# Both heads' sums turned into one tile, two score columns made by ScalarE, and a new list of due times, in an attention and two-layer MLP kernel

## The chip, the cores and the metric

The kernel runs on one core of one Trainium2 chip. The metric is the device time of one execution in microseconds. Engines are named as in the profile: PE is TensorE (PEld its weight loads), DVE is VectorE, ACT is ScalarE, POOL is GpSimd, SP is SyncE, which issues nearly all DMAs here.

## The reference

Attention over 4 batches, 8 heads, 576 positions, head dimension 64, in which scores more than `tau` under the row's maximum are cut off; then two MLP blocks over 2304 tokens (512 wide, 2048 hidden), the first with a squared ReLU, the second with a sigmoid gate.

```python
scores = scale * np.matmul(q, k.transpose(0, 1, 3, 2))
thresh = np.max(scores, axis=-1, keepdims=True) - tau
scores = np.where(scores >= thresh, scores, -1e9)
scores = scores - np.max(scores, axis=-1, keepdims=True)
attn = np.exp(scores)
attn = attn / (np.sum(attn, axis=-1, keepdims=True) + 1e-09)
out = np.matmul(attn, v)
# x = the heads side by side, (2304, 512)
r = np.maximum(x @ w_in, 0.0);  x = (s * (r * r) + b) @ w_out
h = x @ w2_in;  y = (h * (1.0 / (1.0 + np.exp(-1.702 * h)))) @ w2_out
```

## The kernel before

The kernel writes out no order of its own. Its functions hand steps to a planner (`Plan.add`, L133): each step names the engines that may run it with a cost in ns, what it reads and writes, and a due time. `Plan.run` (L175) then lays the steps out one engine at a time by due time and dependence, and buffers of one tag are handed out strictly in the order in which the program asked for them. A step's due time is that of its group plus 100 ns times the group's entry in the list `MOVES` (L53, 663 entries, one a group). TensorE steps of the attention fall due 282.77 us earlier than that (`first`).

Attention runs in 32 head pairs: for each batch (4) and each half of its queries (a unit: 256 queries, in the second unit 64 more, the "last" part), four pairs of heads. The two units of batch 0 are in fp32 and the other six in float16 pieces (value and remainder). A pair has four or five score tiles of 128 queries by 576 keys. For a tile TensorE forms negated scores in two PSUM banks (L563); VectorE takes the minimum `nm` (L587); a step forms `tb`, in float16 tiles two columns, the bound and the bias of the exponential (L601, VectorE; in fp32 tiles L595, one column, GpSimd); ScalarE takes the exponential (L609); VectorE masks it and sums it (L613). Then the tile is turned: fp32 by TensorE (L624) and copies (L393), float16 by two ScalarE and GpSimd steps (L393, L637) and a transposing DMA.

At the end of a pair, `finish_sums` inverts the sums (L649) and spreads them along the queries so that a column of `rs` scales a column of the product with V. In the first 16 pairs this is done through the one PSUM bank of tag `T`: for each head two transpositions (L677) and one copy of 64 partitions (L393), and in units with a last part a third transposition (L683) and two small copies into `rm` (L688). In the other 16 pairs the sums go through DRAM. The product with V (L708) takes the same bank, and VectorE scales it out of PSUM (L723, L729). `finish_last` does the same for the last 64 queries (L749, L757).

The weights of both blocks are converted tile by tile (`convert`, L838): a load of 512 KB into one of three buffers `wst`, a cast (L393 on ScalarE or L387 on VectorE) and a VectorE step that joins two pieces (L851). The first block of 256 tokens goes through the first MLP in fp32 (`pair32`, L1117 to L1133; `rows32`, L1151), as soon as its attention is through; its affine step `s*r*r+b` is a ScalarE step (L1133). The other blocks use float16 pieces (`pair` L1090, `bank` L1183). When attention has ended its memory goes to the second MLP, which forms seven products in place of eight for each 2 by 2 of quarters (`hidden7` L1416, `rows7` L1483 and L1504) over four blocks of 512 tokens and a last one of 256, made of the 64 last queries of each batch. `out` in `rows7` (L1534, L1538) writes the result; for the last block that is two stores for each of two tiles, all issued by SyncE (L415).

Of the kernel before, what the change touches and what calls it, by code (L numbers as in the profile page):

```python
# [121 lines left out]
class Plan:  # L122
# [4 lines left out]
    HOP = {("PE", "PE"): 0.0, ("DVE", "DVE"): 125.0, ("DVE", "SP"): 125.0, ("POOL", "POOL"): 105.0, ("POOL", "SP"): 60.0}  # L127
# [197 lines left out]
def act(cols, psum=False):  # L325
    return cols * 0.834 + (53.0 if psum else 93.0)
# [12 lines left out]
class Kernel:  # L339
# [229 lines left out]
    def tile_step(self, p, i):  # L569
# [22 lines left out]
        if plain:  # L592
            add(
                {"POOL": 360.0},
                lambda _: nc.gpsimd.tensor_scalar(tb(), nm.ap, self.under, None, ALU.add), [nm], [both],  # L595
                prio=self.plan.prio - KN["tb"] * pace,
            )
        else:
            add(
                {"DVE": Shared(200.0)},  # L600
                lambda _: nc.vector.tensor_scalar(both.ap, self.offs, nm.ap, None, ALU.add), [nm], [both],  # L601
                prio=self.plan.prio - KN["tb"] * pace,
            )
# [38 lines left out]
    def finish_sums(self, p):  # L642
# [8 lines left out]
        p["rs"] = rs = self.at("rs", [P, n], F32)  # L651
        if p["last"]:
            p["rm"] = rm = self.at("rm", [P, H2], F32)
        if p["spread"]:
# [7 lines left out]
            for t, part in ((rs, main), (p.get("rm"), last))[: 1 + p["last"]]:  # L662
                cols = t.shape[1]
                for h in range(2):
                    self.load(
                        lambda t=t, h=h: t[h * H2 : (h + 1) * H2],
                        lambda part=part, h=h, cols=cols: rd[part][h * cols : (h + 1) * cols].partition_broadcast(H2),
                        [(t, h)], H2 * cols * 4, reads=[rd],
                    )
            return  # L670
        for h in range(2):
            rT = self.ps("T", [H2, n])

            def turn(_, h=h, rT=rT):
                for t in range(T):
                    i = T * h + t
                    nc.tensor.transpose(rT[:, t * P : (t + 1) * P], ri[:, i : i + 1].to_broadcast([P, H2]), self.ident)  # L677
            add({"PE": pe(2 * T, P)}, turn, [ri], [rT])
            self.copy(lambda h=h: rs[h * H2 : (h + 1) * H2], lambda rT=rT: rT.ap, [rT], [(rs, h)], n, psum=True, more=90.0)
        if not p["last"]:  # L680
            return
        mT = self.ps("T", [P, P])
        add({"PE": pe(2, P)}, lambda _: nc.tensor.transpose(mT.ap, ri[:, 2 * T : 2 * T + 1].to_broadcast([P, P]), self.ident), [ri], [mT])  # L683

        def pick(_):
            for h in range(2):
                rows = slice(h * H2, (h + 1) * H2)
                nc.scalar.activation(rm[rows], mT[rows, rows], AF.Copy)  # L688
        add({"ACT": 220.0}, pick, [mT], [rm])
# [9 lines left out]
    def finish_main(self, p):  # L699
# [18 lines left out]
        x, hp = p["rs"], p["hp"]  # L718
        xs = self.x_of(p["unit"])
        if p["unit"] < KN["fu"]:  # L720
            add(
                {"DVE": dve(n, psum=True) + 60},
                lambda _: nc.vector.tensor_tensor(xs[:, hp, :], Up.ap, x.ap, ALU.mult), [Up, x], [(xs, (0, hp))],  # L723
# [5 lines left out]
            lambda _: nc.vector.scalar_tensor_tensor(x.ap, Up.ap, vb[:, sc : sc + 1], x.ap, ALU.mult, ALU.mult),  # L729
            [Up, vb, x], [x],  # L730
        )
        self.split(
            lambda: xs[:, 0, hp, :], lambda: xs[:, 1, hp, :], lambda: x.ap, [x], [(xs, (0, hp)), (xs, (1, hp))], n, on=None,
        )

    def finish_last(self, p):
# [7 lines left out]
        mT, rm = self.ps("T", [P, H2]), p["rm"]  # L744

        def mix(_):
# [10 lines left out]
            lambda _: nc.vector.scalar_tensor_tensor(xm.ap, mT.ap, sc(), rm.ap, ALU.mult, ALU.mult),  # L757
            [mT, rm] + [vb] * (not p["f32"]), [xm],
# [346 lines left out]
    def pair32(self, u, jp):  # L1105
# [22 lines left out]
        if jp % 2 == 0:  # L1128
            u["g"].append(Buf(self.wp, "g", [P, CH, n], F32, KN["g"]))
        g, k = u["g"][-1], 2 * (jp % 2)  # L1130
        add(
            {"ACT": act(512) + 186},
            lambda _: nc.scalar.activation(  # L1133
                g[:, k : k + 2, :].rearrange("p a b -> p (a b)"), gt.ap, AF.Identity, bias=self.b_ap, scale=self.s_ap
            ),
            [gt, self.scal], [(g, k)],
        )
# [619 lines left out]
```

## Time and profile before

| | before |
|---|---|
| median of 3 runs | 1010.17 us (1006.05 to 1010.31) |
| the profiled execution | 1013.42 us, its span 1011.5 us |
| mean granted TensorE clock | 0.994 |
| busy: TensorE, its weight loads | 971.5 us (96%), 755.0 us (75%) |
| busy: VectorE, ScalarE, GpSimd | 763.6 us (75%), 659.1 us (65%), 251.9 us (25%) |
| chain that ended last | TensorE 74%, VectorE 12%, DMA 6%, ScalarE 5% |

A share of the whole span mixes stages: attention, first MLP and second MLP overlap and have different limits. So the rows further below take the span in stretches, and name what TensorE waited for in each.

### The profile page before, as it was taken

The numbers are of one execution on the slowest core, as the hardware profiler recorded it, in microseconds if no ns is written. First come the engines' busy times: TensorE is split into PE (matmuls) and PEld (weight loads), VectorE is DVE, ScalarE is ACT, GpSimd is POOL, SyncE is SP. The second block draws the span as 40 slices with busy tenths as digits, with TensorE's granted clock in tenths as the row PEclk, the third lists the DMA queues.
The fourth block names the chain that finished last, engine by engine and source line by source line (L and its number), as shares of the span: only waits on it lengthen the run. The fifth ranks groups of instructions, "written<-read, shape, count | busy, mean of one in ns | idle before, by whom it ended". The sixth has DMA issues, their size and how long they took to land.

```text
span 1011.5 us, 22501 instructions
## 1 busy us (share of the span) xinstructions
PE 971.5 (96%) x8649; PEld 755.0 (75%) x8649; DVE 763.6 (75%) x1752; ACT 659.1 (65%) x1349; POOL 251.9 (25%) x362
## 2 busy tenths in 40 slices
PE   6889997999999999999999999999999999999997
PEld 3455665777788777788778888887687687687695
DVE  6989788887687775686665698989859577859665
ACT  5778875597675665776556588787448266547464
POOL 2101134335344544334453101210302000201001
PEclk9999999999999999999999999999999999999999
DMA  7877276785678666667655346601011000010000
GB/s 262 290 267 234 83 150 150 150 194 122 121 147 197 157 136 130 139 143 150 119 128 101 93 137 206 222 12 42 2 42 43 12 32 19 25 43 21 22 23 22
DMA packets 173067, 115.93 MB, mean 115 GB/s; under 512 B 136536, under 2 KB 149920, under 8 KB 172960
## 3 DMA queue, kind: packets, MB, share of 16 engines
q1 hardware_dynamic: 172960, 114.50, 44.0%
q8 instruction: 68, 1.11, 0.5%
q14 instruction: 39, 0.32, 0.1%
HBM read 72.62 MB, written 10.00 MB: 82 GB/s over the span
## 4 chain that ended last, share of the span: by engine, by line
PE 74%; DVE 12%; DMA 6%; ACT 5%; issue 2%; SPq 1%; POOL 0%; DVEq 0%; ACTq 0%
PE a L1483 9%; PE a L1416 9%; PE yy L1183 9%; PE yy L1090 7%; PE S L563 7%; PE y L1090 5%; PE T L708 5%; PE a L1504 3%; PE d L1504 3%; PE y L1183 3%; PE yy L1416 3%; PE y L1151 2%; PE d L1416 2%; DMA wst<-in_moe_w_in 2%; DVE l L967 2%
## 5 line engine op out<-in xcount | busy, mean ns | idle before, releaser
L637 POOL TENSOR_TENSOR p<-e,p 128x512 f16<-128x512 f32 x108 | 129.1, 1195 | 203.9 <-ACT p L393 150.2
L1090 PEld LDWEIGHTS <-wb 128*128 128x128 f16 x1536 | 148.8, 98 | 27.8 <-issue 10.0
L1183 PEld LDWEIGHTS <-wb 128*128 128x128 f16 x1536 | 147.4, 98 | 25.9 <-issue 9.0
L1416 PEld LDWEIGHTS <-l 128*128 128x128 f16 x1680 | 150.7, 98 | 18.8 <-issue 1.5
L1183 PE MATMUL yy<-g,wb 128*128 128x256 f16 x1248 | 145.8, 273 | 0.7 <-ACT gt L1097 0.7
L587 DVE TENSOR_REDUCE nm<-S 128x1 f32<-128x576 f32 x144 | 104.5, 750 | 42.7 <-PE S L563 42.3
L613 DVE SCALAR_TENSOR_TENSOR e<-S,tb,e 128x576 f32<-128x576 f32 x144 | 114.6, 812 | 27.0 <-ACT e L609 25.7
L609 ACT ACTIVATE e<-S,tb 128x576 f32<-128x576 f32 x108 | 76.4, 735 | 59.5 <-DVE tb L601 56.3
L1416 PE MATMUL a<-xs,l 128*128 128x256 f16 (+1 forms) x960 | 109.5, 262 | 1.1 <-ACT wb L1428 1.1
L1090 PE MATMUL yy<-xs,wb 128*128 128x256 f16 x888 | 107.1, 275 | 1.0 <-ACT gt L1208 1.0
L393 ACT ACTIVATE p<-e 128x576 f16<-128x576 f32 x108 | 73.0, 679 | 38.4 <-DMA PT<-p 21.6
L411 POOL TENSOR_TENSOR gt<-gt 128x256 f32<-128x256 f32 (+1 forms) x23 | 18.8, 822 | 267.9 <-DVE gt L411 200.7
L1090 PE MATMUL y<-xs,wb 128*128 128x256 f16 x648 | 77.2, 273 | 2.4 <-ACT gt L1097 1.2
L1504 PEld LDWEIGHTS <-g 128*128 128x128 f16 x714 | 69.5, 98 | 10.1
L395 ACT ACTIVATE g<-gt 128x256 f16<-128x256 f32 (+2 forms) x137 | 49.4, 394 | 30.7 <-DVE gt L411 19.8
L563 PE MATMUL S<-kk,qa 64*128 64x288 f32 (+1 forms) x320 | 55.3, 449 | 8.4 <-ACT kk L448 5.7
L563 PE MATMUL S<-kk,qb 64*128 64x288 f32 (+1 forms) x320 | 58.6, 462 | 3.1 <-DVE e L613 3.0
L1428 ACT ACTIVATE wb<-a 128x256 f32<-128x256 f32 (+1 forms) x120 | 41.4, 357 | 30.2 <-PE a L1416 28.1
L967 DVE SCALAR_TENSOR_TENSOR g<-gt,g 128x256 f16<-128x256 f32 (+1 forms) x133 | 58.0, 466 | 2.7 <-ACT g L395 2.5
L1340 ACT ACTIVATE gt<-wb,x2h 128x256 f32<-128x256 f32 (+2 forms) x80 | 44.4, 577 | 10.4 <-DVE wb L1435 9.7
L851 DVE SCALAR_TENSOR_TENSOR wb<-wst,tw 128x512 int32<-128x512 int32 x64 | 45.3, 719 | 5.2 <-ACT tw L393 4.7
L1483 PE MATMUL a<-wb,wst 128*128 128x512 f16 x216 | 48.9, 380 | 0.0
(202 smaller groups left out, 1786.1 us busy)
## 6 DMA issues: line engine op xcount, KB each, us to landing
wst<-in_moe_w_in SPq DMA_DIRECT2D x32, 512.0 KB, 4.8
wst<-in_moe_w_out SPq DMA_DIRECT2D x32, 512.0 KB, 4.5
rv<-in_v SPq DMA_DIRECT2D x32, 320.0 KB, 3.4
kk<-in_k SPq DMA_DIRECT2D x32, 288.0 KB, 2.9
qb<-in_q SPq DMA_DIRECT2D x16, 288.0 KB, 3.3
yd<-gt SPq DMA_DIRECT2D x18, 256.0 KB, 2.6
wb<-yd SPq DMA_DIRECT2D x16, 256.0 KB
out<-gt SPq DMA_DIRECT2D x16, 256.0 KB, 2.0
```

Source lines behind the costliest of these rows:

```text
L393: nc.scalar.activation(dst(), src(), AF.Copy)
L563: nc.tensor.matmul(Sp[to, half, :HALF], q[h][r, qcols], k[r, h * HALF : (h + 1) * HALF])
L587: {"DVE": 668.0}, lambda _: nc.vector.tensor_reduce(nm.ap, Sv(), AX.XY, ALU.min), [Sp], [nm],
L609: lambda _: nc.scalar.activation(ev(), Sv(), AF.Exp, bias=nm.ap if plain else nb(), scale=-1.0), [Sp, biased], [e],
L613: lambda _: nc.vector.scalar_tensor_tensor(ev(), Sv(), tb(), ev(), ALU.is_le, ALU.mult, accum_out=p["acc"][:, i, 0:1]),
L637: nc.gpsimd.tensor_tensor(p16[:, S + H2 :], e[:, :MAIN], p16[:, :MAIN], ALU.subtract)
L967: lambda _: nc.vector.scalar_tensor_tensor(lo(), src(), by(), hi(), ALU.mult, ALU.subtract),
L1090: nc.tensor.matmul(hps[:, h, :], W[:, i, j, kk * P : (kk + 1) * P], x[:, k, kk, :], start=t == 0, stop=t == len(terms) - 1,)
L1183: nc.tensor.matmul(yp[:, h, :], self.W[0, 1, c][:, i, j, i0 * P : (i0 + 1) * P], u["g"][c][:, k, j, :], start=t == 0, stop=t == len(terms) ...
L1416: nc.tensor.matmul(to(bank), W[:, u, m, j, kk * P : (kk + 1) * P], y[:, v, z, kk, :], start=n == 0 and not more, stop=n == 5, skip_group_c ...
L1483: nc.tensor.matmul(Y[r].ap, g[:, k, z, f // 2, cols], self.W[1, 1, c][:, w, f, :], start=(c, f, k, w) == (flat[0], 0, 0, 0), stop=(c, f, k ...
L1504: nc.tensor.matmul(region(bank), g[:, u, z, rows], W[:, v, y, j, :], start=i == 0 and not more, stop=i == last, skip_group_check=True,)
```

## The change

1. Sums. In the first 16 pairs both heads go into one tile of the bank `T`, head 0 in partitions 0 to 63 and head 1 in 64 to 127, with plain products by the identity in place of transpositions. The last part's column goes into 64 more columns of the same tile. One copy takes all of it to `rs`, which is 320 columns wide where there is a last part, and `rm` is gone. In the other 16 pairs the four loads from DRAM go into that one tile.
2. The two-column step of the float16 score tiles is an activation on ScalarE (Identity, bias `nm`).
3. The affine step of `pair32` may be planned on ScalarE or on GpSimd.
4. In the last block the second of each two stores is issued by ScalarE's queue.
5. The planner counts 100 ns from a ScalarE step to the next; before, it counted 160.
6. The 663 entries of `MOVES` are new. Those of the first 32 weight tiles, with the due times that come out:

| weight tiles (group) | due before, us | due after, us |
|---|---|---|
| first matrix, tiles 0 to 11 (432 to 443) | -5 to 92 | -288 to -51 |
| second matrix, tiles 0 to 4 (444 to 448) | 74 to 200 | -442 to -185 |
| second matrix, tile 5 (449) | -74 | 361 |
| second matrix, tile 6 (450) | 144 | -163 |
| second matrix, tiles 7 to 14 (451 to 458) | 42 to 146 | 156 to 537 |
| second matrix, tile 15 (459) | 58 | -540 |
| first matrix, tiles 12 to 15 (460 to 462, 464) | 17 to 123 | 74 to 439 |

The diff, without the list:

```diff
-    HOP = {("PE", "PE"): 0.0, ("DVE", "DVE"): 125.0, ...}
+    HOP = {("PE", "PE"): 0.0, ("ACT", "ACT"): 100.0, ("DVE", "DVE"): 125.0, ...}
...
             add(
-                {"DVE": Shared(200.0)},
-                lambda _: nc.vector.tensor_scalar(both.ap, self.offs, nm.ap, None, ALU.add), [nm], [both],
+                {"ACT": 210.0},
+                lambda _: nc.scalar.activation(both.ap, self.offs, AF.Identity, bias=nm.ap), [nm], [both],
                 prio=self.plan.prio - KN["tb"] * pace,
             )
...
-        p["rs"] = rs = self.at("rs", [P, n], F32)
-        if p["last"]:
-            p["rm"] = rm = self.at("rm", [P, H2], F32)
+        rs = self.at("rs", [P, n + H2 * p["last"]], F32)
+        p["rs"] = rs
...
-        for h in range(2):
-            rT = self.ps("T", [H2, n])
-
-            def turn(_, h=h, rT=rT):
+        wide = n + H2 * p["last"]
+        rT = self.ps("T", [P, wide])
+
+        def turn(_):
+            for h in range(2):
+                rows = slice(h * H2, (h + 1) * H2)
                 for t in range(T):
                     i = T * h + t
-                    nc.tensor.transpose(rT[:, t * P : (t + 1) * P], ri[:, i : i + 1].to_broadcast([P, H2]), self.ident)
-            add({"PE": pe(2 * T, P)}, turn, [ri], [rT])
-            self.copy(lambda h=h: rs[h * H2 : (h + 1) * H2], lambda rT=rT: rT.ap, [rT], [(rs, h)], n, psum=True, more=90.0)
-        if not p["last"]:
-            return
-        mT = self.ps("T", [P, P])
-        add({"PE": pe(2, P)}, lambda _: nc.tensor.transpose(mT.ap, ri[:, 2 * T : 2 * T + 1].to_broadcast([P, P]), self.ident), [ri], [mT])
-
-        def pick(_):
-            for h in range(2):
-                rows = slice(h * H2, (h + 1) * H2)
-                nc.scalar.activation(rm[rows], mT[rows, rows], AF.Copy)
-        add({"ACT": 220.0}, pick, [mT], [rm])
+                    nc.tensor.matmul(rT[rows, t * P : (t + 1) * P], ri[:, i : i + 1].to_broadcast([P, H2]), self.ident)
+                if p["last"]:
+                    nc.tensor.matmul(rT[rows, n:], ri[:, 2 * T : 2 * T + 1].to_broadcast([P, H2]), self.ident[:, rows])
+        add({"PE": (pe(2 * T + p["last"], P), 60.0)}, turn, [ri], [rT])
+        self.copy(lambda: rs.ap, lambda: rT.ap, [rT], [rs], wide, psum=True, more=20.0)
...
-        add(
-            {"ACT": act(512) + 186},
...
+        def line(e):
+            to = g[:, k : k + 2, :].rearrange("p a b -> p (a b)")
+            if e == "POOL":
+                nc.gpsimd.tensor_scalar(to, gt.ap, self.s_ap, self.b_ap, ALU.mult, ALU.add)
+            else:
+                nc.scalar.activation(to, gt.ap, AF.Identity, bias=self.b_ap, scale=self.s_ap)
+        engines = {"ACT": act(512) + 186, "POOL": pool(512, True)}
+        add({e: engines[e] for e in (("ACT",), ("ACT", "POOL"), ("POOL",))[KN["lp2"]]}, line, [gt, self.scal], [(g, k)])
...
-            for part, dst in blk["rows"][r * half // P + t]:
-                self.load(lambda dst=dst: dst, lambda part=part: K[r][part], [], P * DM * 4, reads=[K[r]])
+            for i, (part, dst) in enumerate(blk["rows"][r * half // P + t]):
+                if n == MAIN or i == 0:
+                    self.load(lambda dst=dst: dst, lambda part=part: K[r][part], [], P * DM * 4, reads=[K[r]])
+                else:
+                    add(
+                        {"ACT": dma(P * DM * 4, 520.0)}, lambda _, dst=dst, part=part: nc.scalar.dma_start(dst, K[r][part]), [K[r]], []
+                    )
```

## Rows read from the trace of the kernel before

**Rows 1.** Busy time by stretch: start:end, length, then each engine's busy us, clock, DMA.

```profile
0.00:25.00 25.00, 15.61 (x56) 8.82 (x57) 16.50 (x38) 13.20 (x23) 5.88 (x18) 1.00 0.75 260
25.00:65.00 40.00, 34.00 (x227) 19.16 (x226) 34.83 (x73) 30.05 (x63) 5.39 (x17) 0.96 0.81 279
65.00:125.00 60.00, 55.83 (x420) 37.89 (x419) 48.69 (x121) 50.49 (x106) 8.54 (x24) 1.00 0.56 184
125.00:175.00 50.00, 42.72 (x360) 31.43 (x359) 44.06 (x111) 35.24 (x62) 17.77 (x28) 0.97 0.65 143
175.00:550.00 375.00, 371.35 (x3689) 294.48 (x3689) 272.49 (x630) 245.41 (x436) 161.93 (x228) 1.00 0.68 143
550.00:700.00 150.00, 145.51 (x1359) 128.40 (x1357) 124.15 (x241) 115.94 (x240) 17.39 (x13) 1.00 0.37 117
700.00:1006.50 306.50, 306.45 (x2550) 234.79 (x2547) 222.16 (x543) 168.75 (x425) 35.01 (x36) 1.00 0.08 27
```

**Rows 2.** Waits of TensorE, 0 to 175 us: total us, times, longest us.

```profile
PE S L563 <- ACT kk L448: 5.7, 1, 5.7
PE S L563 <- DVE e L613: 4.6, 6, 1.5
...
PE T L677 <- DVE rs L729: 1.9, 1, 1.9
...
PE T L708 <- ACT rm L688: 0.6, 2, 0.4
```

**Rows 3.** Groups of VectorE, 0 to 65 us: busy us, mean ns, idle before.

```profile
L851 DVE SCALAR_TENSOR_TENSOR wb<-wst,tw 128x512 int32<-128x512 int32 x21 | 14.2, 687 | 2.3 <-ACT tw L393 2.2
L387 DVE CAST tw<-wst 128x512 f16<-128x512 bf16 x8 | 3.6, 449 | 0.0
```

**Rows 4.** Timeline of TensorE, 0 to 30 us: start us, length us, instructions.

```profile
22.04 1.33 PE L563 MATMUL S<-kk,qb 64*128 64x288 f32 x4
...
29.46 0.76 PE L563 MATMUL S<-kk,qa 64*128 64x288 f32 x4
```

**Rows 5.** Groups by form, whole span: busy us, mean ns, idle before.

```profile
L1117 PE MATMUL y<-xs,wb 128*128 128x256 f32 x128 | 30.6, 385 | 1.9 <-DVE n L895 1.9
...
L1208 ACT ACTIVATE gt<-yy,b,y 128x256 f32<-128x256 f32 x26 | 13.3, 557 | 6.1 <-PE yy L1183 5.8 <-DVE b L1070 0.3
...
L677 PE MATMUL T<-ident,ri 128*64 128x128 f32 x64 | 13.0, 287 | 2.8 <-DVE rs L729 1.9 <-DVE ri L649 0.9
...
L393 ACT ACTIVATE rs<-T 64x256 f32<-64x256 f32 x32 | 11.9, 372 | 6.6 <-PE T L677 5.2 <-POOL xs L411 1.0
...
L1133 ACT ACTIVATE g<-gt,scal 128x512 f32<-128x512 f32 x8 | 6.5, 809 | 0.1
...
L688 ACT ACTIVATE rm<-T 64x64 f32<-64x64 f32 x16 | 3.4, 211 | 1.1 <-PE T L683 1.0
...
L683 PE MATMUL T<-ident,ri 128*128 128x128 f32 x8 | 2.4, 298 | 0.3 <-ACT rs L393 0.3
```

**Rows 6.** Timeline of TensorE, 60 to 90 us.

```profile
64.57 0.27 PE L488 MATMUL T<-ident,mx 128*8 128x128 f32 x1
...
71.35 0.38 PE L500 MATMUL T<-dg,ones 8*128 8x8 f32 x2
```

**Rows 7.** Line L601: shortest, median and longest ns; below, who waited (us, times).

```profile
L601 DVE TENSOR_SCALAR tb<-offs,nm x108: 208/221/1168, 120.0 to 549.4; 128x2 f32<-128x2 f32 x108
...
  ACT e L609: 56.3, 34
```

**Rows 8.** Line L601 by stretch, to 550 us: length, VectorE's busy us, clock.

```profile
125.00:175.00 50.00, 3.19 (x11) 0.97 0.65 143
...
sum 550.00, DVE 34.29; mean DVE 11.43
```

**Rows 9.** Timeline of SyncE's queue, 1000 to 1012 us.

```profile
1005.99 2.44 SPq L415 DMA_DIRECT2D out<-gt  x4
```

**Rows 10.** Timeline of TensorE, 120 to 150 us.

```profile
137.85 3.72 PE L1117 MATMUL y<-xs,wb 128*128 128x256 f32 x16 [0.67 <-DVE n L895]
```

More of the change, by code (lines that the diff above doesn't have):

```diff
@@ L122 @@
 class Plan:
-    HOP = {("PE", "PE"): 0.0, ("DVE", "DVE"): 125.0, ("DVE", "SP"): 125.0, ("POOL", "POOL"): 105.0, ("POOL", "SP"): 60.0}
+    HOP = {("PE", "PE"): 0.0, ("ACT", "ACT"): 100.0, ("DVE", "DVE"): 125.0, ("DVE", "SP"): 125.0, ("POOL", "POOL"): 105.0, ("POOL", "SP"): 60.0}
     def __init__(self):
@@ L661, in finish_sums @@
             main, last = slice(0, 2 * n), slice(2 * n, 2 * n + P)
-            for t, part in ((rs, main), (p.get("rm"), last))[: 1 + p["last"]]:
-                cols = t.shape[1]
+            for to, part in ((slice(0, n), main), (slice(n, n + H2), last))[: 1 + p["last"]]:
+                cols = to.stop - to.start
                 for h in range(2):
                     self.load(
-                        lambda t=t, h=h: t[h * H2 : (h + 1) * H2],
+                        lambda to=to, h=h: rs[h * H2 : (h + 1) * H2, to],
                         lambda part=part, h=h, cols=cols: rd[part][h * cols : (h + 1) * cols].partition_broadcast(H2),
-                        [(t, h)], H2 * cols * 4, reads=[rd],
+                        [(rs, (to.start, h))], H2 * cols * 4, reads=[rd],
                     )
             return
-        for h in range(2):
-            rT = self.ps("T", [H2, n])
-            def turn(_, h=h, rT=rT):
+        wide = n + H2 * p["last"]
[3 more added lines that the diff above has]
+                rows = slice(h * H2, (h + 1) * H2)
                 for t in range(T):
                     i = T * h + t
-                    nc.tensor.transpose(rT[:, t * P : (t + 1) * P], ri[:, i : i + 1].to_broadcast([P, H2]), self.ident)
-            add({"PE": pe(2 * T, P)}, turn, [ri], [rT])
-            self.copy(lambda h=h: rs[h * H2 : (h + 1) * H2], lambda rT=rT: rT.ap, [rT], [(rs, h)], n, psum=True, more=90.0)
-        if not p["last"]:
-            return
-        mT = self.ps("T", [P, P])
-        add({"PE": pe(2, P)}, lambda _: nc.tensor.transpose(mT.ap, ri[:, 2 * T : 2 * T + 1].to_broadcast([P, P]), self.ident), [ri], [mT])
-        def pick(_):
-            for h in range(2):
-                rows = slice(h * H2, (h + 1) * H2)
-                nc.scalar.activation(rm[rows], mT[rows, rows], AF.Copy)
-        add({"ACT": 220.0}, pick, [mT], [rm])
+                    nc.tensor.matmul(rT[rows, t * P : (t + 1) * P], ri[:, i : i + 1].to_broadcast([P, H2]), self.ident)
[3 more added lines that the diff above has]
+        self.copy(lambda: rs.ap, lambda: rT.ap, [rT], [rs], wide, psum=True, more=20.0)
     def terms(self, p):
@@ L717, in finish_main @@
             add({"PE": (len(some) * cost + 200.0, 60.0)}, lambda _, some=some: mix(_, some), [V, p["PT"][0], p["PT"][1]], [Up])
-        x, hp = p["rs"], p["hp"]
+        rs, hp = p["rs"], p["hp"]
+        x, some = lambda: rs[:, :n], [(rs, (0, h)) for h in range(2)]
         xs = self.x_of(p["unit"])
@@ L722, in finish_main @@
                 {"DVE": dve(n, psum=True) + 60},
-                lambda _: nc.vector.tensor_tensor(xs[:, hp, :], Up.ap, x.ap, ALU.mult), [Up, x], [(xs, (0, hp))],
+                lambda _: nc.vector.tensor_tensor(xs[:, hp, :], Up.ap, x(), ALU.mult), [Up] + some, [(xs, (0, hp))],
             )
@@ L728, in finish_main @@
             {"DVE": dve(n, psum=True) + 126},
-            lambda _: nc.vector.scalar_tensor_tensor(x.ap, Up.ap, vb[:, sc : sc + 1], x.ap, ALU.mult, ALU.mult),
-            [Up, vb, x], [x],
+            lambda _: nc.vector.scalar_tensor_tensor(x(), Up.ap, vb[:, sc : sc + 1], x(), ALU.mult, ALU.mult),
+            [Up, vb] + some, some,
         )
         self.split(
-            lambda: xs[:, 0, hp, :], lambda: xs[:, 1, hp, :], lambda: x.ap, [x], [(xs, (0, hp)), (xs, (1, hp))], n, on=None,
+            lambda: xs[:, 0, hp, :], lambda: xs[:, 1, hp, :], x, some, [(xs, (0, hp)), (xs, (1, hp))], n, on=None,
         )
@@ L743, in finish_last @@
         sc = (lambda: 1.0) if p["f32"] else (lambda: vb[:, 16 + hp : 17 + hp])
-        mT, rm = self.ps("T", [P, H2]), p["rm"]
+        mT, rs, rm = self.ps("T", [P, H2]), p["rs"], lambda: p["rs"][:, p["n"] :]
         def mix(_):
@@ L756, in finish_last @@
             {"DVE": dve(H2) + 61},
-            lambda _: nc.vector.scalar_tensor_tensor(xm.ap, mT.ap, sc(), rm.ap, ALU.mult, ALU.mult),
-            [mT, rm] + [vb] * (not p["f32"]), [xm],
+            lambda _: nc.vector.scalar_tensor_tensor(xm.ap, mT.ap, sc(), rm(), ALU.mult, ALU.mult),
+            [mT] + [(rs, (p["n"], h)) for h in range(2)] + [vb] * (not p["f32"]), [xm],
         )
@@ L1130, in pair32 @@
         g, k = u["g"][-1], 2 * (jp % 2)
-        add(
-            {"ACT": act(512) + 186},
[L1133 to L1137, printed above, removed]
+        def line(e):
[6 more added lines that the diff above has]
+        add({e: engines[e] for e in (("ACT",), ("ACT", "POOL"), ("POOL",))[KN["lp2"]]}, line, [gt, self.scal], [(g, k)])
     def rows32(self, u, c):
```

72 rows, old and new, of tables (KN, MOVES) are left out of this document.

## Prediction

> **What bounds the kernel now.** I read the table by stage first: busy time of each engine in seven stretches that reach from the first instruction to the last matmul [rows 1]. The reader is to subtract TensorE's busy time from the length of each. From 700 to 1006.5 us it is busy 306.45 of 306.5: no order of the work gains there. From 175 to 550 it lacks 3.65 us, from 550 to 700 4.49 us. From 0 to 175 it lacks 9.39 + 6.00 + 4.17 + 7.28 = 26.84 us. The seven busy times add up to 971.47 us, and the last matmul is followed by 5.0 us of output. So the kernel is bound by TensorE's work, and a change that leaves that work as it is can gain at most the 35 us of idle time, most of it before 175 us.
>
> Then the waits of TensorE in the first 175 us [rows 2]. The first, 5.7 us for the scaled keys, is the start of the kernel and stays. The next, 4.6 us, is for the masked exponentials that VectorE writes; VectorE is busy 16.50, 34.83, 48.69 and 44.06 us of 25, 40, 60 and 50 in the four early stretches [rows 1], so from 25 us on it is the short engine there. Its groups up to 65 us [rows 3] show what stands beside the score tiles: 21 weight tiles are converted (L851, and a cast for eight of them), 17.8 us. Last the timeline of TensorE at the start: four score matmuls take 1.33 us at 22 us and 0.76 us at 29 us [rows 4], so the early matmuls ran at about the lower of the two clock levels (1.2 and 2.4 GHz), though the column of the granted clock reads 1.00 there [rows 1].
>
> **The sums of both heads.** Sixteen of the 32 head pairs (first two batches) turn their sums on TensorE. Before: 64 transpositions (13.0 us busy, 0.203 each), two ScalarE copies per pair (32, 11.9 us) and, for the eight last pairs, one more transposition (0.30 us) and two small picks (16, 3.4 us) [rows 5]. After: 64 fp32 products of 128 columns, 16 of 64 columns, and 16 copies of 256 or 320 columns. No such product is in the trace; the fp32 product of 256 columns at L1117 is two records, 30.6 us over 64 products, 0.478 us, so I take 0.24 for 128 columns and 0.12 for 64: 15.4 + 1.9 = 17.3 us against 13.0 + 2.4 = 15.4. That is +1.9 us on the critical engine, in 23 to 281 us. Bounds: nothing, if the two heads' products share the array as the products with V do, to +4 us, if each costs a quarter more. The copy lies between 0.37 us (256 columns, no pointer) and 0.56 (256 columns, two pointers) [rows 5]; at 0.42 the 16 cost 6.7 us where copies and picks cost 15.3, so ScalarE gains 8.6 us, off the path. Of the waits, the 0.6 us for the pick (L708 behind rm) goes [rows 2]; the 1.9 us for the PSUM bank held by the previous product (T behind rs) stays, since the bank is still one. Sum +1.3 us, bounds -2.5 to +4. The other sixteen pairs keep their four loads, now into one tile: 0. The reciprocal tile now holds the last part too and is held until that part is used; two score tiles lie between, so I cost it at nothing; if that cover fails it is one more wait such as the 1.9 us.
>
> A row shows that a transposition and a product are not the same thing to TensorE: the transposition at L488 is one record and the product at L500 two [rows 6]. The Trainium skill, TensorE: Matmul & The Clock Gate, section Terms, says that the transposing mode is four times as fast for fp32, which speaks against this step. By a factor of four on the row's 0.203 us the 64 products would cost 52 us in place of 13.0, 39 us more. The trace does not bear it out: 0.24 against 0.203.
>
> **Bias and bound on ScalarE.** Of the 144 score tiles, 108 are float16. Their VectorE step (L601, two columns) has a median of 0.221 us and a longest of 1.168 [rows 7] and takes 34.3 us in all [rows 8]. After the change VectorE is rid of all of it. ScalarE gets 108 activations of two columns with a bias pointer. Nearest rows: a plain 64-column activation 0.211 us, and 0.557 us for 256 columns with two pointers against 0.372 for 256 columns with none [rows 5], about 0.09 a pointer. So 0.21 - 0.05 + 0.09 = 0.25 us, 27 us in all, bounds 0.16 to 0.37, 17 to 40 us. Where it lies: nearly all but 11 of the tiles are in 175 to 550 us, where VectorE goes from 272 to about 242 us of 375 and ScalarE from 245 to about 269: neither becomes the bound, and TensorE lacks only 3.65 us [rows 1]. ScalarE already waits 56.3 us, 34 times, for L601 at the exponential [rows 7]; it will now wait for the minimum one step earlier, with the same PSUM evictions of the MLP queued behind it. I take 0 there, bounds -3.6 to +4. From 125 to 175 us 11 of these steps cost VectorE 3.2 us [rows 8] while it is busy 44 of 50 us and TensorE lacks 7.3: I take -2, bounds -3.2 to 0.
>
> **GpSimd as a choice** for eight affine steps (0.81 us each, 6.5 us of ScalarE [rows 5]): no early wait of TensorE of any size ends on them, so 0, bounds -1 to +1.
>
> **The last output.** Four issues on the SyncE queue take 2.44 us, 0.61 each [rows 9]. The second of each pair goes to ScalarE's queue, where nothing is left to hold it: -0.6 us, bounds -0.6 to 0 (nothing, if another block ends last).
>
> **The new order.** It leaves TensorE's matmuls as they are and moves their idle time. In the list the first twelve tiles of the first matrix and the first five of the second fall due at -442 to -51 us instead of -5 to 200; from the sixth tile of the second matrix on, most fall due at 117 to 537. Their staging buffer is taken in the order of the program, so one low tile holds back those behind it. Before, 21 tiles were converted up to 65 us; I expect 17 or so. Four fewer, at 0.69 us (L851) and for 8 of 21 a 0.45 us cast [rows 3], are some 3.4 us less on the engine that is short, before the first token block is through; the shorter start also brings the higher clock sooner. I take -5 us, between 0 and -15 (half of the 21 us of early idle time without the start, and some of the slow matmuls). For 550 to 700 us I take -1, bounds -4 to +4.
>
> **Sum.** +1.3 + 0 - 2 + 0 - 0.6 - 5 - 1 = -7.3 us on the profiled execution's 1013.42 us, which gives 1006.1. That execution is 3.25 us above the median of the runs shown, 1010.17 (1006.05 to 1010.31); against the median it is 1002.9, and I say 1002.5.
>
> **Rivals.**
> Nothing moves: VectorE stays full up to 65 us whatever is converted when, and the two gains are eaten by the dearer products. 1010.2 + 1.3 - 0.6 - 1 = 1010, within half a percent of before (about what a measurement of this kernel can tell from no change). For it: the idle time is spread over many waits, the largest 5.7 us. Against: 17.8 of VectorE's first 51 busy us are conversions and casts that can move [rows 3]. Chance 0.25.
>
> A larger gain: the early order keeps TensorE fed, the early idle time falls by 13 us and 4 to 6 us of slow matmuls run at the higher level: 1010.2 - 19 = 991. For it: 1.33 against 0.76 us a step [rows 4]. Against: VectorE's work there does not shrink. Chance 0.17.
>
> Slower, by one mechanism: the last four tiles of the first weight matrix. They stand in the staging order behind all of the second matrix, and fall due at 74 to 439 us instead of 17 to 123. Before, the last products of the first block, which read them, ran from 137.85 us [rows 10], while VectorE was full. If these tiles come later than that, the last two hidden pairs, and all that needs the first block's rows, wait. Decisive is whether those products start after 145 us; a delay of 25 us, covered by some 12 us of the next block's products, costs 13 us more: 1002.5 + 13 = 1015.5, with more delay 1020. For it: early windows have no other matmuls in stock. Against: an idle queue starts the load whatever its due time. Chance 0.16.
>
> The products of the identity cost as four transpositions do: 64 x 0.203 x 3 = 39 us on TensorE, 1002.5 + 39 = 1041. Against: the 0.24 us above. Chance 0.02; the page named above is the one that gives it.
>
> **How the numbers follow.** My forecast (997 to 1005) has 0.40, the larger gain 0.17, no change 0.25, slower 0.18. Faster by over half a percent (under 1005.1) thus 0.57, within it 0.25, slower (over 1015.2) 0.18. The range leaves out the best of the larger gain and the worst of the slower cases: 987 to 1017.
>
> **What would show it.** In the changed kernel's profile: TensorE's busy time within 5 us of 971.5, less where slow matmuls have gone; idle time before 175 us near 20 us in place of 26.8; no L601 on VectorE, and 108 two-column activations of 0.2 to 0.3 us; 17 or so conversions up to 65 us; sixteen copies of the sums at about 0.4 us; the end 4.4 us after the last matmul. It is wrong if the idle time before 175 us does not fall, if the gain appears after 700 us, or if the identity's products take over 0.4 us each.

## The result and the profile after

| | before | after |
|---|---|---|
| median of the runs, us | 1009.9 (1006.05 to 1010.31) | 999.95 (999.49 to 1001.92) |
| ratio to before | 1 | 0.9914 (95% interval 0.9894 to 0.9934) |
| measured once more beside before | 1011.39 | 1001.26, ratio 0.9907 (0.9883 to 0.9932) |
| span of the profiled execution, us | 1011.5 | 997.6 (once more: 1000.3) |
| busy: TensorE, VectorE, ScalarE, us | 971.5, 763.6, 659.1 | 968.7, 735.8, 668.8 |

The kernel became 0.9% faster; the forecast was 1002.5 us. The granted TensorE clock doesn't account for that: the executions in which its mean was 0.998 took 1005.63 to 1010.79 us before, and 999.49, 999.68 and 1000.16 after. Here are the first six of the seven stretches for the changed kernel, first execution (start:end, length, busy us of TensorE, its weight loads, VectorE, ScalarE and GpSimd, clock, DMA). In the seventh, from 700 us to the last matmul, TensorE is full as before.

```profile
0.00:25.00 25.00, 15.44 (x63) 8.85 (x63) 16.33 (x37) 14.66 (x25) 6.02 (x19) 1.00 0.79 271
25.00:65.00 40.00, 34.40 (x252) 21.46 (x251) 36.22 (x85) 29.74 (x61) 5.72 (x16) 1.00 0.87 287
65.00:125.00 60.00, 59.76 (x476) 43.49 (x477) 49.33 (x113) 46.39 (x94) 13.59 (x28) 1.00 0.51 169
125.00:175.00 50.00, 44.84 (x370) 33.08 (x369) 45.86 (x113) 36.74 (x73) 19.96 (x30) 0.97 0.80 167
175.00:550.00 375.00, 372.87 (x3805) 296.80 (x3804) 250.07 (x525) 263.91 (x520) 165.45 (x233) 1.00 0.71 144
550.00:700.00 150.00, 148.37 (x1303) 126.94 (x1301) 131.03 (x262) 120.08 (x256) 27.04 (x17) 1.00 0.32 110
```

And the second profiled execution of the same kernel:

```profile
0.00:25.00 25.00, 13.50 (x63) 7.95 (x65) 16.54 (x38) 14.99 (x26) 6.02 (x19) 0.93 0.78 272
25.00:65.00 40.00, 33.51 (x240) 21.22 (x239) 34.37 (x80) 28.58 (x59) 5.25 (x16) 0.96 0.85 279
65.00:125.00 60.00, 59.65 (x477) 43.22 (x475) 48.89 (x116) 45.44 (x91) 13.71 (x28) 1.00 0.51 168
125.00:175.00 50.00, 44.17 (x376) 32.71 (x375) 46.04 (x112) 37.39 (x75) 19.86 (x30) 1.00 0.77 165
175.00:550.00 375.00, 372.55 (x3797) 296.35 (x3796) 250.15 (x526) 263.10 (x520) 167.20 (x233) 1.00 0.73 145
550.00:700.00 150.00, 147.19 (x1303) 127.00 (x1302) 130.60 (x257) 119.29 (x254) 27.03 (x17) 1.00 0.32 110
```

Read against [rows 1], by length minus TensorE's busy time. From 65 to 125 us the idle time fell from 4.17 to 0.24 us, and to 0.35 in the second execution. From 125 to 175 it went from 7.28 to 5.16 and 5.83, from 175 to 550 from 3.65 to 2.13 and 2.45, from 550 to 700 from 4.49 to 1.63 and 2.81. The first 65 us gained nothing: 15.39 before, 15.16 and 17.99 after. There the two executions of one program differ by 2.8 us, in which the granted clock differs too (1.00 and 1.00 against 0.93 and 0.96), so a single profile can't tell a gain of 2 us there. On the first pair of profiles the account closes: TensorE busy 2.8 us less, idle before its last matmul 10.6 less, and 0.5 less behind it, together 13.9. With the second execution of the changed kernel it is 5.2, 5.6 and 0.4, together 11.2. So idle time is between half and three quarters of the gain. The shorter busy time stands in the score matmuls: 102.9 us before, 99.8 and 97.9 after.

The waits of TensorE in the first 175 us (us in total, times, longest), of which the keys' 5.7 us stay:

```profile
PE S L567 <- ACT kk L452: 5.7, 1, 5.7
PE TP L628 <- ACT PT L397: 5.5, 5, 1.6
PE TP L628 <- DVE e L617: 2.1, 1, 2.1
PE S L567 <- DVE e L617: 1.6, 3, 1.0
```

Of those in [rows 2], the one for the masked exponentials at the scores fell from 4.6 to 1.6 us (2.6 in the second execution), and the two at the bank `T` (behind `rs` and `rm`, 2.5 us) are gone. Another grew: the turning of fp32 tiles behind ScalarE's copies (TP behind `PT`) was 2.3 us and is 5.5. The first block's fp32 products, line L1117 before and L1115 after, show what came earlier (shortest, median, longest ns; first and last start). Of before, then of after:

```profile
L1117 PE MATMUL y<-xs,wb x128: 378/380/484, 64.7 to 147.0; 128*128 128x256 f32 x128
```

```profile
L1115 PE MATMUL y<-xs,wb x128: 379/379/483, 59.8 to 130.8; 128*128 128x256 f32 x128
```

They start 5 us and end 16 us sooner (3 and 14 in the second execution), which gives TensorE more work in the stretch from 65 to 125 us. The changed steps themselves, in groups by form (busy us, mean ns, idle before):

```profile
L605 ACT ACTIVATE tb<-offs,nm 128x2 f32<-128x2 f32 x108 | 30.7, 288 | 22.9 <-DVE nm L591 22.7
L613 ACT ACTIVATE e<-S,tb 128x576 f32<-128x576 f32 x108 | 79.0, 736 | 4.2 <-POOL p L642 0.2
L682 PE MATMUL T<-ident,ri 128*64 128x128 f32 x128 | 13.6, 304 | 0.2 <-DVE ri L653 0.2
L684 PE MATMUL T<-ident,ri 128*64 128x64 f32 x32 | 4.4, 220 | 0.0
L397 ACT ACTIVATE rs<-T 128x320 f32<-128x320 f32 x8 | 3.5, 436 | 4.8 <-PE T L684 3.1 <-issue 1.8
L397 ACT ACTIVATE rs<-T 128x256 f32<-128x256 f32 x8 | 3.0, 372 | 1.7 <-PE T L682 1.7
```

### The profile page after: what moved, and what is told of

Same layout as the page of the kernel before. It is cut to its first block, busy times and chain, and to the rows that moved or that the text cites. A ratio compares the mean times of both kernels' runs of the same rounds, so it can differ in the third digit from the quotient of the medians.

```text
span 997.6 us, 22675 instructions
## 1 busy us (share of the span) xinstructions
PE 968.7 (97%) x8737; PEld 759.1 (76%) x8737; DVE 735.8 (74%) x1643; ACT 668.8 (67%) x1420; POOL 263.1 (26%) x368
## 4 chain that ended last, share of the span: by engine, by line
PE 51%; DVE 4%; DMA 4%; ACT 2%; issue 1%; SPq 1%; POOL 1%; POOLq 0%; DVEq 0%; ACTq 0%
PE a L1483 9%; PE a L1416 9%; PE yy L1183 6%; PE yy L1088 4%; PE a L1504 4%; PE d L1504 4%; PE yy L1416 3%; PE y L1088 3%; PE d L1416 2%; PE y L1183 2%; PE S L567 2%; DMA PT<-p 2%; PE y L1416 1%; PE T L705 1%; DVE l L965 1%
## 5 line engine op out<-in xcount | busy, mean ns | idle before, releaser
L1416 PEld LDWEIGHTS <-l 128*128 128x128 f16 x1680 | 151.0, 98 | 20.6 <-issue 1.8
L1088 PE MATMUL yy<-xs,wb 128*128 128x256 f16 x888 | 104.7, 273 | 0.0
L397 ACT ACTIVATE p<-e 128x576 f16<-128x576 f32 x108 | 72.8, 678 | 40.0 <-DMA PT<-p 29.8
L613 ACT ACTIVATE e<-S,tb 128x576 f32<-128x576 f32 x108 | 79.0, 736 | 4.2 <-POOL p L642 0.2
L1340 ACT ACTIVATE gt<-wb,x2h 128x256 f32<-128x256 f32 (+1 forms) x80 | 44.7, 578 | 25.9 <-DVE wb L1435 22.1
L965 DVE SCALAR_TENSOR_TENSOR g<-gt,g 128x256 f16<-128x256 f32 (+1 forms) x133 | 53.8, 433 | 4.7 <-ACT g L399 4.3
```

Source lines behind the costliest of these rows:

```text
L397: nc.scalar.activation(dst(), src(), AF.Copy)
L613: lambda _: nc.scalar.activation(ev(), Sv(), AF.Exp, bias=nm.ap if plain else nb(), scale=-1.0), [Sp, biased], [e],
L965: lambda _: nc.vector.scalar_tensor_tensor(lo(), src(), by(), hi(), ALU.mult, ALU.subtract),
L1088: nc.tensor.matmul(hps[:, h, :], W[:, i, j, kk * P : (kk + 1) * P], x[:, k, kk, :], start=t == 0, stop=t == len(terms) - 1,)
L1416: nc.tensor.matmul(to(bank), W[:, u, m, j, kk * P : (kk + 1) * P], y[:, v, z, kk, :], start=n == 0 and not more, stop=n == 5, skip_group_c ...
```

## The experiments

There are two kinds. Some kernels let the planner lay out the steps anew. In the others the order is held: the planner sees the steps, costs and list of one kernel, and only what a planned step issues is exchanged at its place. Code below is shortened. The expectations name the theories: A, the list of due times carries the gain; B, the single turn and copy of the sums; C, list and steps belong together; D, the two-column step; E and F, two reasons for D.

### Steps and list exchanged, laid out anew

The edits with the old list, and the new list without the edits:

```diff
 # e1: the changed kernel
-MOVES = [the new list]
+MOVES = [the list of the kernel before]
 # e2: the kernel before
-MOVES = [its list]
+MOVES = [the new list]
```

> All edits of the change, with the list of due times of the kernel before. Theory A (the gain is the new list's: which steps come early; the edits are worth 2 us at most): 1008 to 1012 us, idle time of TensorE before 175 us near 26 us. Rival B (the gain is the edits': one turn of the PSUM bank and one copy shorten every early head pair, whatever the list): 1000 to 1004 us, that idle time near 20 us. Rival C (list and edits belong together, a list fits only the steps for which it was made): 1010 to 1025 us.

> The kernel before with the new list alone, no other edit. Theory A: 1000 to 1004 us, idle time of TensorE before 175 us near 21 us. Rival B: 1007 to 1011 us. Rival C: 1010 to 1025 us.

1030.05 us, ratio 1.0205 (1.0174 to 1.0237), and 1099.03 us, ratio 1.0879 (1.0846 to 1.0912). A and B fall. C has the direction, but both kernels are slower than its 1010 to 1025 us. The stretches from 175 to 700 us, of e1 and then of e2:

```profile
175.00:550.00 375.00, 367.19 (x3686) 291.54 (x3687) 255.79 (x537) 261.90 (x518) 164.74 (x230) 1.00 0.69 147
550.00:700.00 150.00, 139.09 (x1262) 121.11 (x1260) 114.89 (x217) 101.50 (x204) 12.53 (x8) 0.97 0.32 112
```

```profile
175.00:550.00 375.00, 336.16 (x3151) 262.71 (x3149) 238.68 (x538) 214.90 (x386) 139.11 (x199) 0.95 0.59 126
550.00:700.00 150.00, 131.15 (x1234) 105.62 (x1235) 100.02 (x210) 86.69 (x162) 44.13 (x55) 0.93 0.49 121
```

TensorE, which lacked 3.65 and 4.49 us there before [rows 1], lacks 7.8 and 10.9 in e1 and 38.8 and 18.9 in e2. Most of the added idle time stands where TensorE was full before, not in the start that the prediction weighed: ahead of 175 us it is 28.8 and 29.8 us, against 26.8. In e2 TensorE is also busy 26.8 us longer in all, and its granted clock is 0.95 and 0.93 in these two stretches.

### One number of the planner

The steps and the list are those of the changed kernel; only the planner's guess for the time between two ScalarE steps is put back.

```diff
-    HOP = {("PE", "PE"): 0.0, ("ACT", "ACT"): 100.0, ...}
+    HOP = {("PE", "PE"): 0.0, ...}
```

> The changed kernel with every step as it is; only the planner's number for the time from one ScalarE step to the next is 160 ns again in place of 100, so that the planner lays the same steps out anew under the same list. If the list's due times carry the gain by what they put early (theory A): 999 to 1004 us. If the list fits only the very layout for which it was made (theory C): 1015 to 1060 us, with the loss spread over the first 700 us.

1057.65 us, ratio 1.047 (1.0446 to 1.0494). Here are the same two stretches again, and the longest waits of TensorE:

```profile
175.00:550.00 375.00, 354.99 (x3485) 281.39 (x3484) 235.37 (x489) 241.22 (x473) 152.46 (x213) 0.97 0.64 135
550.00:700.00 150.00, 128.49 (x1219) 109.03 (x1217) 101.58 (x194) 94.72 (x192) 28.41 (x29) 0.95 0.45 133
```

```profile
PE T L705 <- DMA PT<-p: 10.5, 2, 7.8
PE S L567 <- DVE e L617: 7.3, 9, 2.4
```

TensorE is idle 20.0 and 21.5 us in place of 2.1 and 1.6. The chip does the same work, apart from a handful of steps that the planner gave to another engine (ScalarE 1413 instructions in place of 1420, GpSimd 373 in place of 368); the layout costs 57 us. So here the due times of the list work only in the layout for which they were chosen, and what a single group's shift does (the prediction's weight tiles) can't be read off the list.

### The edits in the old order, and the old work in the new order

To see what the edits are worth, the order must therefore be held. These are four kernels, with the exchanged part of each:

```diff
 # f1, at the place of the planned VectorE step (order of before)
-nc.vector.tensor_scalar(both.ap, self.offs, nm.ap, None, ALU.add)
+nc.scalar.activation(both.ap, self.offs, AF.Identity, bias=nm.ap)
 # f2: all products by the identity at the first head's turn, one copy at its copy;
 #     the second turn, its copy, the third turn and the picks issue nothing
 # f3: f1 and f2, and the last block's second stores on nc.scalar
 # f4 (order of after)
-nc.scalar.activation(both.ap, self.offs, AF.Identity, bias=nm.ap)
+nc.vector.tensor_scalar(both.ap, self.offs, nm.ap, None, ALU.add)
-one copy of 128 partitions
+a copy of each 64 partitions, of the main and of the last part
-nc.scalar.dma_start(dst, K[r][part])
+nc.sync.dma_start(dst, K[r][part])
```

> The kernel before with its order kept step for step; only the two-column step of the float16 score tiles is an activation of ScalarE, at the place at which VectorE's was planned. Theory D (the step is better on ScalarE in any order, since there it neither waits behind VectorE's long steps nor behind GpSimd): 1003 to 1006 us, ScalarE's idle time ahead of the exponentials down from 56 to under 30 us. Theory C (it pays only in an order made for it): 1008 to 1014 us.

> The kernel before with its order kept; both heads' sums (and the last part) are formed at the place of the first head's turn, with one copy at the place of its copy, and the second turn, its copy and the picks are left out. Theory B (one turn of the bank shortens the early pairs): 1004 to 1007 us, and idle time of TensorE before 175 us down from 26.8 to about 22. Theory A (nothing on the path): 1008 to 1011 us.

> The two former together with the last block's second stores on ScalarE's queue, in the order of the kernel before (the affine step stays on ScalarE). If the edits carry the gain by themselves: 999 to 1003 us. If they carry half and the order the rest: 1003 to 1007. If only the order counts: 1008 to 1011.

> The changed kernel with its order kept: the two-column step on VectorE, the one copy cut into two (four with a last part) at the same place, the last block's stores all on SyncE's queue. With the step alone on VectorE it was 1006.4 us. Theory A (copies and stores are worth nothing but the last issue): 1006 to 1008 us. Theory B: 1009 to 1012 us, no faster than before, so that the new order by itself gives nothing.

| | order of before | order of after |
|---|---|---|
| old work | 1 | f4 0.9992 (0.9975 to 1.0010), 1009.2 us |
| two-column step on ScalarE | f1 0.9994 (0.9976 to 1.0013), 1009.97 us | |
| one turn and copy of the sums | f2 1.0023 (1.0011 to 1.0036), 1012.02 us | |
| all of these edits | f3 1.0025 (0.9999 to 1.0051), 1012.63 us | after 0.9914, 0.9907 |

In f4 the products by the identity stay, with one turn of the bank for both heads and the affine step where the new layout put it; in f3 the affine step stays on ScalarE. The rest is the full exchange. What the products by the identity are worth in the new order is not measured: the kernel with transpositions in their place gave no time. Within these limits the edits alone give nothing, the order alone gives nothing, and both give 0.9%. The gain is their joint effect, which none of the prediction's terms was. The single turn by itself made the kernel slower in the old order, by 0.1 to 0.4%.

The early stretch shows one part of it in both orders. From 65 to 125 us, of f2, f3 (the fastest of its ten executions, 5 us under their median) and f4:

```profile
65.00:125.00 60.00, 57.85 (x464) 39.69 (x464) 50.28 (x123) 49.32 (x97) 9.53 (x25) 1.00 0.55 181
```

```profile
65.00:125.00 60.00, 57.98 (x464) 40.01 (x463) 49.27 (x121) 49.44 (x99) 8.47 (x24) 1.00 0.54 180
```

```profile
65.00:125.00 60.00, 58.73 (x470) 42.23 (x469) 47.58 (x109) 47.42 (x98) 13.40 (x28) 1.00 0.50 167
```

The single turn takes the idle time there from 4.17 to 2.15 and 2.02 us in the old order (f1, without it, has 3.92). The new order with the copies cut up has 1.27. The changed kernel has 0.24 and 0.35, but g4 below, which is the same up to the last stores, has 1.63: executions of one program differ by 1.4 us here too, and what the single copy does in this stretch can't be told. So the sums carry some 2 of the up to 3.9 us gained in that stretch, and the order some more. In the old order f2 gives back a part of it elsewhere (5.62 us idle from 550 to 700 where before lacked 4.49); why its median is 2 us longer all the same, no profile settles.

### The two-column step in the new order

These are the changed kernel with its order held and the step issued to VectorE (e3), and the step issued to both engines, VectorE's into a tile that nobody reads (g2):

```diff
 # e3
-lambda _: nc.scalar.activation(both.ap, self.offs, AF.Identity, bias=nm.ap)
+lambda _: nc.vector.tensor_scalar(both.ap, self.offs, nm.ap, None, ALU.add)
 # g2
 nc.scalar.activation(both.ap, self.offs, AF.Identity, bias=nm.ap)
+nc.vector.tensor_scalar(self.spare, self.offs, nm.ap, None, ALU.add)
```

> The changed kernel with its order kept step for step; only the two-column step of the float16 score tiles is issued to VectorE again, at the place at which ScalarE's step was planned. Theory A: 1000 to 1002 us, TensorE's idle time from 175 to 550 us still under 4 us, since TensorE is full there. Rival D (this step is a main part of the gain, since on VectorE it sometimes waits over a microsecond): 1004 to 1008 us with over 6 us of idle time there.

> The changed kernel with its order kept; beside ScalarE's two-column step VectorE does the same step too, into a scratch tile that nobody reads. So the chain of a score tile stays as it is, and VectorE has its 108 short steps back. If VectorE's own time is what the step costs (theory E): 1004 to 1007 us. If the hop through VectorE's queue and back is what it costs, ScalarE standing idle ahead of the exponential (theory F): 999.5 to 1002 us.

e3: 1006.42 us, ratio 0.9969 (0.9953 to 0.9984). g2: 1003.25 us, ratio 0.9920 (0.9898 to 0.9942). In the new order the step's place is worth 0.9969 - 0.9914 = 0.55%, 5.5 us, more than half of the gain, and the intervals don't touch. Rival D has the time; its over 6 us of idle time from 175 to 550 us did not come (3.86). With VectorE's 108 steps back beside it, 0.06% of that is lost, within the intervals. The time of g2 lies between the ranges of E and F, but its ratio is that of the changed kernel: VectorE's own time is not what the step cost, and E falls as the main cause. ScalarE's groups in e3, and the groups in g2:

```profile
L613 ACT ACTIVATE e<-S,tb 128x576 f32<-128x576 f32 x108 | 78.2, 737 | 64.5 <-DVE tb L605 60.1 <-DVE t L998 1.8 <-PE T L684 1.4
```

```profile
L616 ACT ACTIVATE e<-S,tb 128x576 f32<-128x576 f32 x108 | 79.0, 736 | 4.4 <-POOL p L645 0.4
L606 DVE TENSOR_SCALAR spare<-offs,nm 128x2 f32<-128x2 f32 x108 | 35.0, 324 | 1.0
L605 ACT ACTIVATE tb<-offs,nm 128x2 f32<-128x2 f32 x108 | 30.8, 289 | 24.5 <-DVE nm L592 24.4
```

ScalarE stands 64.5 us ahead of the exponential where the step is VectorE's, and 22.9 + 4.2 us ahead of step and exponential where it is its own. That speaks for F. In the old order the same exchange left it standing longer. Of before, then of f1:

```profile
L609 ACT ACTIVATE e<-S,tb 128x576 f32<-128x576 f32 x108 | 76.4, 735 | 59.5 <-DVE tb L601 56.3 <-PE T L708 2.6 <-DVE n L922 0.3
```

```profile
L609 ACT ACTIVATE e<-S,tb 128x576 f32<-128x576 f32 x108 | 76.0, 731 | 1.5
L601 ACT ACTIVATE tb<-offs,nm 128x2 f32<-128x2 f32 x108 | 30.2, 289 | 40.2 <-DVE nm L587 40.0
```

It waits 41.7 us in place of 59.5 before, 18 less where the new order has 37 less; f1's step stands at the place planned for VectorE, and ScalarE's queue comes to it before its minimum is there (40.0 us). TensorE's stretches in e3 from 125 us on:

```profile
125.00:175.00 50.00, 42.99 (x356) 31.50 (x354) 47.32 (x121) 32.71 (x58) 19.19 (x29) 0.97 0.74 156
175.00:550.00 375.00, 371.14 (x3749) 294.30 (x3748) 269.87 (x618) 242.84 (x424) 166.11 (x235) 1.00 0.71 145
550.00:700.00 150.00, 147.25 (x1345) 128.75 (x1343) 128.89 (x249) 118.42 (x249) 27.05 (x17) 1.00 0.32 110
```

Its idle time there is 7.0, 3.9 and 2.8 us, 13.6 in all, against 8.9 and 11.1 in the changed kernel. How the step's 5.5 us come about through ScalarE's waits is not settled: TensorE itself names no wait of that size behind the exponentials.

### Copies and stores

```diff
 # g3: only the copies of f4;  g4: only the stores of f4
```

> The changed kernel with its order kept; the one copy of the sums is two copies of 64 partitions (four with a last part) at the same place, ScalarE 8.6 us longer in all. Theory A: 999.5 to 1001 us. If the single copy is worth the 2.8 us by which old work in the new order was slower than the step alone on VectorE: 1002 to 1004 us.

> The changed kernel with its order kept; the last block's four stores all issued on SyncE's queue. The prediction's price: 0.6 us more, 1000.5 us, the end 5.0 us after the last matmul in place of 4.4; no time that the medians can tell. If the second queue is worth nothing, the end stays at 4.4 us.

g3: 1005.11 us (999.52 to 1007.39), ratio 0.9941 (0.9916 to 0.9966); g4: 1002.6 us, ratio 0.9919 (0.9900 to 0.9938). The copies may be worth up to 5 us or nothing: their interval reaches into that of the changed kernel, and the six executions lie 8 us apart. The stores can't be told from it in time. So the part of the gain that e3 keeps, 0.3%, is not divided further: the intervals of e3 and f4 overlap too. The last lines of the two timelines show them, of after and then of g4 (start, length):

```profile
990.28 2.78 PE L1504 MATMUL a<-wb,g 128*128 128x256 f16 x24
...
992.61 1.76 SPq L419 DMA_DIRECT2D out<-gt  x2
992.64 1.77 ACTq L1542 DMA_DIRECT2D out<-gt  x2
```

```profile
991.37 2.78 PE L1504 MATMUL a<-wb,g 128*128 128x256 f16 x24
...
995.55 0.59 SPq L1542 DMA_DIRECT2D out<-gt  x1
```

From the last matmul to the end it is 997.6 - 993.06 = 4.54 us with two queues (4.62 in the second execution) and 999.0 - 994.15 = 4.85 with one.

### The changed kernel again

> The changed kernel once more, nothing altered, so that the kernels of the new order have a neighbour measured beside as many executions as they had. If the first four executions stand for it: 999.5 to 1001 us. If single calls differ by more than their executions: 1001 to 1003 us, and then the stores on SyncE's queue (1002.6) and the step taken twice (1003.3) cost less than the difference to the first four suggests.

1001.26 us beside 1011.39 of the kernel before: the ratio 0.9907 repeats 0.9914, and the absolute time is 1.3 us higher. So ratios to the kernel before are compared above where the times lie close. By 0.9907 the step's place would be worth 0.62% in place of 0.55.

## Why the prediction was right, and where its steps failed

**The bound.** This was right in the main: TensorE's busy time went from 971.5 to 968.7 and 966.3 us, the idle time fell ahead of 700 us, and TensorE stayed full after it. But "most of it before 175 us" is only half true: from 65 to 175 us 6.0 and 5.3 us were gained, from 175 to 700 us 4.4 and 2.9, and ahead of 65 us none. The idle time ahead of 175 us, forecast at near 20 us in place of 26.8, came to 20.6 and 24.2. The second busy time is 5.2 us less, just over the 5 us that were allowed.

**The sums.** The copies were priced at 6.7 us and took 6.5. The products were priced at 17.3 us. Their two groups show 13.6 and 4.4 us, but the groups interleave and overlapped time counts in both. Together TensorE is busy on them for 14.5 us (14.1 in the second execution), against 15.4 for the transpositions. All instructions on the tile `ri`, of which TensorE's are these, of before and then of after:

```profile
0.00:285.00 285.00, 15.40 (x72) 7.08 (x72) 5.46 (x32) 0.98 0.67 181
```

```profile
0.00:280.00 280.00, 14.52 (x160) 11.20 (x160) 5.43 (x32) 0.99 0.71 187
```

That does not make them cheaper: a busy time also holds the end of a turn's last matmul, and that overlaps what follows (71.86 against 71.79 us below). From the start of a turn to the start of what follows is the better measure, here of a pair with a last part:

```profile
70.82 0.71 PE L682 MATMUL T<-ident,ri 128*64 128x128 f32 x6
...
71.79 1.15 PE L567 MATMUL S<-kk,qa 64*128 64x288 f32 x6
```

This is 0.97 us for the one turn, where the three turns before took 0.31, 0.25 and 0.16 (at 102.94, 104.58 and 76.81 us). So the products are dearer, as forecast. The 1.9 us wait behind the bank's previous product, which was to stay, is gone; it stayed in f2 and f3, so the new order took it away and not the single turn. The net of +1.3 us agrees with the time of f2, 2.0 us more than before, while f2's stretch from 65 to 125 us has 2.0 us less idle time. The rival by which the products cost as four transpositions do is excluded: that would have been 52 us. The Trainium skill, TensorE: Matmul & The Clock Gate, section Terms, gives that factor of four for fp32; this trace does not show it.

**Bias and bound.** An activation took 0.288 us where 0.25 was forecast. The Trainium skill, ScalarE: Activation LUTs, section What ACT_TABLE_LOAD costs, has about 0.28 us for two columns with a bias pointer, and the trace agrees. From 125 to 175 us, where -2 was taken, e3 is idle 1.2 to 1.9 us longer than the changed kernel, near the forecast. From 175 to 550 us, where 0 was taken, it is 1.4 to 1.7 us: this term was mis-sized, and with it the whole, -2 for a step that is worth 5.5 us in the new order and nothing in the old. That neither engine "becomes the bound" looked at shares of busy time; g2 shows that the time was not in VectorE's work. That it was in ScalarE's wait for VectorE's queue is what e3's 64.5 us speak for, without settling it. The 56.3 us that ScalarE waited [rows 7] were on the page and were costed at nothing.

**The new order.** The size was near, the mechanism was wrong. VectorE converted 22 weight tiles up to 65 us (21 in the second execution), not 17, against 21 before [rows 3]:

```profile
L849 DVE SCALAR_TENSOR_TENSOR wb<-wst,tw 128x512 int32<-128x512 int32 x22 | 15.1, 685 | 1.1 <-ACT tw L397 1.0
```

and f4 shows that the order with the old work is no faster than before (0.9992). The term of -5 us was given to the order alone and belongs to order and edits together. The higher clock did not come sooner by the order either. At the start four score matmuls take 1.33 us for the last time at 22.0 us before [rows 4] and at 21.8 us after, and 0.76 us from 24.7 to 25.4 us on in f2, f3 and the changed kernel alike (its second execution has an earlier spell of it at 14 us, and so has e1 with the old list). That 1.33 us is the lower level is borne out: at 46.5 us before, where the granted clock is 0.57, four take 1.33 us again.

**The last output.** It is 0.5 us less between the two profiles, 0.3 by g4, where 0.6 was forecast.

**GpSimd.** It took seven of the eight affine steps; none of TensorE's waits names them. This was forecast at nothing; no kernel changed it alone, so it is not shown.

**The rivals.** The slower one (the first matrix's last four tiles) did not happen: the products that need them ran from 127 us and ended at 131, not later than 147. "Nothing moves" is what the edits and the order each give alone. The larger gain wanted 13 us less idle time early; 6.3 and 2.7 came. The forecast came out right in part by luck, by a sum whose two largest terms were sized wrongly in opposite directions: the order's -5 was too good for the order, and the step's -2 too little for the step.

## What to carry to other kernels

Where a planner lays out the order, cost an edit with the order held and again laid out anew: here the same edits gave nothing in one order, 0.9% in another and lost 2% laid out under a list made for other steps. An engine's wait ahead of a long step for a tiny step on another engine is a candidate for cost, even where both engines have time to spare; here putting the tiny step on the waiting engine paid in the order made for it, and not in the other. Look at two executions of one kernel before a difference of 2 to 3 us in one stretch is explained. And don't add the busy times of two groups of matmuls that interleave: measure from start to start.

## What was not expected of the hardware

A two-column step takes 0.278 to 0.313 us on ScalarE and 0.199 to 1.184 us on VectorE in the same place of the same order:

```profile
L605 ACT ACTIVATE tb<-offs,nm x108: 278/286/313, 121.3 to 531.6; 128x2 f32<-128x2 f32 x108
```

```profile
L605 DVE TENSOR_SCALAR tb<-offs,nm x108: 199/223/1184, 121.5 to 536.6; 128x2 f32<-128x2 f32 x108
```

(shortest, median and longest ns; the changed kernel, then e3). Why VectorE's longest is five times its median, no run settles.
